# RetNet attention and a PReLU MLP in one kernel: masks and carries moved to ScalarE and GpSimd, one PReLU issued earlier, the copies of the running sums one gap later

## The chip, the cores and the metric

The kernel runs on one core of a Trainium2 chip. The core has TensorE (matmuls, called PE in the profile; PEld are its weight loads), VectorE (DVE), ScalarE (ACT), GpSimd (POOL) and SyncE (SP), whose queue issues nearly all the DMAs here. Each engine works through its own instructions in order; an instruction that must wait for another engine holds up everything behind it on its own. The metric is device time in microseconds of one execution.

## What is computed

The reference has two blocks. The first is a retention layer: 8 batches, 8 heads, 576 positions, head size 64. The second is an MLP over the 4608 tokens of 512 features that come out of it, with 2048 hidden features and a PReLU whose slope differs for each hidden feature.

```python
scores = scale * np.matmul(q, k.transpose(0, 1, 3, 2))
Dmat = np.where(rel >= 0, gamma[:, None, None] ** rel[None, :, :], 0.0)
ret = scores * Dmat[None, :, :, :]
return np.matmul(ret, v).astype(np.float32)
...
h = x @ w_in
g = np.maximum(h, 0.0) + alpha * np.minimum(h, 0.0)
return (g @ w_out).astype(np.float32)
```

Everything is 32-bit floating point. `Dmat` is a causal decay, a power of the head's `gamma` in the distance of two positions.

## The kernel before

**Attention in chunks.** The decay factors into a power for the row and one for the column, so q and v are scaled once, and a sequence of 576 is cut into 9 chunks of 64. Inside a chunk the scores are multiplied by a triangular 0/1 `mask`. What earlier chunks contribute is kept as a 64x64 state per head: the products of k and v of one chunk, summed over the chunks before it with a decay. Values are mask part plus state part.

**Batches after the first** are done by pair of heads, four pairs a batch. A pair has five steps: `scale_pair` (GpSimd scales q at L500, ACT scales v at L505), `transposes` (DVE, L511), `pair_scores` (PE L528, copies of q on ACT L531, masks on DVE L536), `pair_states` and `pair_values`. `pair_states` makes the products `pu` on PE (L547), copies the even ones on ACT (L552), forms the running sums `su` on DVE (L554, L558, L560), and in its last lines copies the sums into `vn` on ACT (L563), from where `pair_values` (PE L574) multiplies them. `su` has the one buffer of tag `kT`.

**The first batch** is done in three parts over all heads at once, two of four chunks and one of one chunk (`PARTS`). Part two is part number 1 in the code. For each part: `part_scale` (GpSimd, L595; argument 1 is q, 2 is v), `part_transposes` (PE L615, copies mostly on ACT L622; 0 is k, 1 is q), `part_scores` (PE L634, two masked copies out of PSUM on DVE at L638), `part_states` (PE L651, sums on DVE L661), `part_carry` (DVE L665: the last sum with the decay of a chunk, into the next part), `part_values` (PE L677 and L688, copies on ACT L693 and L695).

**The weights** come in 32 pieces of 512 KB, in the order in which the hidden units need them: for each of 8 units two pieces of `w_in` and two of `w_out`. The kernel reads both 32-bit halves of 64-bit numbers and builds 32-bit numbers from them. `piece_in` is the ACT half (L274, L276), into one of three buffers `wa`. `piece_out` is three DVE steps (L285, L288, L290) through one PSUM bank and an addition on GpSimd (L292); after it, `fetch` issues DMAs for a later piece, up to seven ahead, into a buffer whose old piece must have had its addition.

**The MLP** goes over blocks of 256 tokens. Each unit has two halves: hidden features (`ph`), PReLU, and the product with `w_out` (`po`, in `mlp_out`). Blocks 0 and 1 are done plainly: `plain_unit` is 16 matmuls (L395) into the single bank `psh0` and two Relus on ACT (L399, L401); `plain_relu` combines them on DVE (L411, two instructions), which also frees the bank; `mlp_out` is eight matmuls (L374). The other 16 blocks use a seven-product scheme of Strassen's kind (L439 and L359), whose weight sums `combine` makes on GpSimd (L302).

**The order of the work.** From the start up to the end of blocks 0 and 1, the order of instructions on each engine is that of the source (`tc.manual_schedule`). First come the parts of batch 0, with pieces of weights and the first four plain units between them. The names `part_...`, `piece_...`, `plain_unit(kb, i)` and `mlp_out` stand there one under another, and each puts its instructions at the tail of its engines' queues. Then a loop over twelve plain units has two places, the gaps, in which one entry of the list `steps` is worked off: "t" is `transposes`, "s" `pair_scores`, "u" `pair_states`, "p" `scale_pair`, "v" `pair_values` and the loads of the pair after the next. The list for a pair is:

```python
steps += [(("s", n),), (("u", n),), (("p", n + 1),), (("v", n), ("t", n + 1)), ()]
```

and the body of the loop, per unit: `plain_unit`, `plain_relu`, first gap, `piece_in`, `piece_out`, `mlp_out`, `combine`, `piece_in`, second gap, `piece_out`, `combine`. In the third of these units the first gap gets "s" and the second "u"; in later ones the entries follow on. After the loop, at about 160 us, the hand-written order is closed, and the rest (the other 24 attention pairs and the other blocks) is ordered by the framework from its source order and dependences.

Of the kernel before, what the change touches and what calls it, by code (L numbers as in the profile page):

```python
# [14 lines left out]
ALU = mybir.AluOpType  # L15
# [3 lines left out]
def kernel(  # L19
# [10 lines left out]
    nc = tc.nc  # L30
# [3 lines left out]
    P = 128  # L34

    NPAIR = H // 2
    C = 64
# [94 lines left out]

    def load_part(x):
        j0, j1 = PARTS[x]
        for i, src, eng in ((0, k, nc.sync), (1, q, nc.scalar if x == 0 else nc.sync),
                            (2, v, nc.sync)):
            for m in range((j1 - j0 + 1) // 2):
                s0 = (j0 + 2 * m) * C
                rows = min(P, j1 * C - s0)
                eng.dma_start(part[x][i][0:rows, m],  # L140
                              src[0, :, s0:s0 + rows].rearrange("h p d -> p h d"))

    load_part(0)
    a16 = const.tile([NFC, P], FP32, name="a16")
# [134 lines left out]
    def piece_out(n):  # L279
        for _ in range(min(n, len(half_done))):  # L280
            at, a, lo, hi, t = half_done.pop(0)
            dst = pieces[at][1]

            c = ps_h.tile([P, 2, HM], INT32, tag="psh1", name=f"wc_{at}")
            nc.vector.tensor_scalar(c.bitcast(FP32), a, HI_MIN, HI_MAX, ALU.max, ALU.min)  # L285


            nc.vector.tensor_scalar(c, c, 3, 0x3FFFFFF8,  # L288
                                    ALU.logical_shift_left, ALU.bitwise_and)
            nc.vector.scalar_tensor_tensor(out=dst.bitcast(INT32), in0=hi, scalar=-0x40000000,  # L290
                                           in1=c, op0=ALU.bitwise_and, op1=ALU.bitwise_or)
            nc.gpsimd.tensor_tensor(out=dst.bitcast(INT32), in0=dst.bitcast(INT32), in1=lo,  # L292
                                    op=ALU.add)
            free.append(t)
            fetch(at + 1 + AHEAD)
# [55 lines left out]
    def mlp_out():  # L351
        kb, i, g = pend.pop(0)
        if kb in PLAIN:
            return plain_out(kb, i, g)
        if i == 0:
            acc[kb] = [ps_o.tile([P, 2, HM], FP32, tag=f"pso{n}", name=f"po{n}_{kb}")
                       for n in range(4)]
        for n, (x, y) in enumerate(PROD):
            nc.tensor.matmul(acc[kb][n // 2][:, n % 2, :], g[:, x, :], w_out[i][:, y, :],  # L359
                             start=(i == 0 and n % 2 == 0),  # L360
                             stop=(i == NU - 1 and (n % 2 == 1 or n == 6)),
                             skip_group_check=True)
        if i == NU - 1:
            out_block(kb, acc.pop(kb))
# [42 lines left out]
    def plain_relu():  # L407
        kb, i, g, ph = relus.pop(0)
        for x in range(2):
            fc = x * NU + i  # L410
            nc.vector.scalar_tensor_tensor(  # L411
                out=g[:, 2 * x:2 * x + 2].rearrange("p m t -> p (m t)"),
                in0=g[:, 4 + 2 * x:6 + 2 * x].rearrange("p m t -> p (m t)"),
                scalar=nalpha[:, fc:fc + 1], in1=ph[:, x], op0=ALU.mult, op1=ALU.add)
        pend.append((kb, i, g))
# [125 lines left out]
    def pair_states(n, kn, vn):  # L541
        c = pairs[n][1]
        ps = [ps_tile([P, NM - 1, D], f"pu{p2}_{n}") for p2 in range(2)]
        for j in range(NJ - 1):
            for h2 in range(2):
                x = (h2, 1 - h2)[j % 2]
                nc.tensor.matmul(ps[j % 2][half(x), j // 2], kn[half(1 - h2), j],  # L547
                                 vn[half(1 - h2), h2, j], start=True, stop=True)
        su = attn.tile([P, S], FP32, tag="kT", name=f"su_{n}")[:, 0:S - D].rearrange(
            "p (j d) -> p j d", d=D)  # L550
        g1, g2 = gch[:, 0, c:c + 1], gch[:, 1, c:c + 1]
        nc.scalar.copy(su[:, 0::2], ps[0])  # L552
        for h2 in range(2):
            nc.vector.scalar_tensor_tensor(  # L554
                out=su[half(h2), 1::2], in0=su[half(h2), 0::2], scalar=g1[half(h2)],
                in1=ps[1][half(1 - h2)], op0=ALU.mult, op1=ALU.add)
        for j in range(3, NJ - 1, 2):
            nc.vector.scalar_tensor_tensor(out=su[:, j], in0=su[:, j - 2], scalar=g2,  # L558
                                           in1=su[:, j], op0=ALU.mult, op1=ALU.add)
        nc.vector.scalar_tensor_tensor(out=su[:, 2::2], in0=su[:, 1:NJ - 3:2], scalar=g1,  # L560
                                       in1=ps[0][:, 1:], op0=ALU.mult, op1=ALU.add)
        for h2 in range(2):
            nc.scalar.copy(vn[half(h2), h2, 1:], su[half(h2)])  # L563

# [24 lines left out]
    def part_scale(x, i):  # L589

        j0, j1 = PARTS[x]
        t = part[x][i]
        for m in range((j1 - j0 + 1) // 2):
            rows = min(P, (j1 - j0) * C)
            nc.gpsimd.tensor_tensor(  # L595
                out=t[0:rows, m], in0=t[0:rows, m],
                in1=tp[0:rows, i - 1, m, :, None].to_broadcast([rows, H, D]), op=ALU.mult)
# [26 lines left out]
    def part_scores(x):  # L624
        at = tat[x] = (mlp.tile([P, 8 * P], FP32, tag="g", name=f"pa_{x}") if x == 0 else
                       room(4, 0, 4)).rearrange("p (h n) -> p h n", h=2)
        banks = part_banks(x, 2 if x == 0 else None, "ps")
        kT, qT = tT[x, 0], tT[x, 1]
        for m in range(2):
            for c in range(NPAIR):  # L630
                for p2 in range(2):
                    for h2 in range(2):
                        j = chunk(2 * m + p2)
                        nc.tensor.matmul(banks[h2][half(p2), (2 * c + m) * C:(2 * c + m + 1) * C],  # L634
                                         kT[half(h2), c, j], qT[half(h2), c, j],
                                         start=True, stop=True)
        for h2 in range(2):
            nc.vector.tensor_tensor(  # L638
                out=at[:, h2].rearrange("p (n s) -> p n s", s=C),
                in0=banks[h2].rearrange("p (n s) -> p n s", s=C),  # L640
                in1=mask[:, None, :].to_broadcast([P, 8, C]), op=ALU.mult)

    def part_states(x):
        kn, vn = part[x][0], part[x][2]
# [17 lines left out]
            was = sums[x][j]  # L662

    def part_carry(x):
        nc.vector.tensor_tensor(out=carry[x + 1], in0=sums[x][3],  # L665
                                in1=gch[:, 2, :, None].to_broadcast([P, NPAIR, D]), op=ALU.mult)

    def part_values(x):
# [75 lines left out]
    part_scale(0, 2)  # L744
    part_scores(0)
    part_states(0)
    part_carry(0)
    piece_in(2)
    piece_out(2)
    part_values(0)  # L750
    aps = ps_a.tile([P, NFC], FP32, tag="psa", name="aps")
    nc.tensor.transpose(aps, a16, ident[0:NFC, 0:NFC])
    nc.vector.tensor_copy(alpha, aps)
    nc.vector.tensor_scalar(nalpha, alpha, -1.0, None, ALU.mult)
    piece_in(3)
    piece_out(1)
    part_scale(1, 1)
    piece_out(2)
    part_scale(1, 2)
    piece_in(1)  # L760
    plain_unit(0, 0)
    plain_relu()
    part_transposes(1, 0)
    part_transposes(1, 1)
    piece_out(1)
    mlp_out()
    piece_in(1)
    piece_out(1)
    part_scores(1)
# [28 lines left out]

    turned, mts = {}, {}

    def step(what, n):
        if what == "p":
            scale_pair(n)
        elif what == "t":
            turned[n] = transposes(n)
        elif what == "s":
            mts[n] = pair_scores(n, *turned.pop(n))
        elif what == "u":  # L810
            pair_states(n, loaded[n][0], loaded[n][3])
        elif what == "v":
            pair_values(n, loaded[n][3], mts[n])
            del loaded[n]
            loaded[n + 2] = load_pair(n + 2)
# [2 lines left out]
    last = 2 * NPAIR - 1  # L818
    steps = [(("t", NPAIR),)]
    for n in range(NPAIR, last + 1):  # L820
        steps += [(("s", n),), (("u", n),), (("p", n + 1),), (("v", n), ("t", n + 1)), ()]

    def gap():
        for x in steps.pop(0) if steps else ():
# [28 lines left out]
    for n, (b, c) in enumerate(pairs):  # L853
        if n <= last:
            continue
        if n == last + 1:
            pop_units(1)
        if n + 1 < len(pairs) and n + 1 not in loaded:
            loaded[n + 1] = load_pair(n + 1)
        kn, _, _, vn = loaded[n]  # L860
        share = -(-len(queue) // (NPAIR - c))
        cuts = [(share + i) // 3 for i in range(3)][::-1]
        kT, qT = turned.pop(n)
        mt = pair_scores(n, kT, qT)
        pop_units(cuts[0])
        pair_states(n, kn, vn)
        pop_units(cuts[1])
        if n + 1 < len(pairs):
            scale_pair(n + 1)
            turned[n + 1] = transposes(n + 1)  # L870
        pair_values(n, vn, mt)
        del loaded[n]
        pop_units(cuts[2])
        if c == NPAIR - 1:
            enqueue(b)
# [31 lines left out]
```

## Time and profile before

| | |
|---|---|
| median of 4 runs | 1029.34 us (1028.92 to 1029.66) |
| the profiled execution's own time | 1029.66 us |
| its span in the profile | 1027.9 us |
| PE busy | 1008.6 us, 98% of the span |
| DVE busy | 772.0 us, 75% |
| ACT busy | 266.8 us, 26% |
| POOL busy | 173.3 us, 17% |
| PE busy, 20 to 48 us | 24.59 us of 28.00 |
| PE busy, 48 to 77 us | 29.00 us of 29.00 |
| PE busy, 77 to 125 us | 46.47 us of 48.00 |
| PE busy, 125 to 160 us | 35.00 us of 35.00 |
| PE busy, 160 to 860 us | all of it |

A line of the timeline reads: start in us, time from the first to the last of the group in us, engine, line of the source, operation, what is written and read, shapes, count; in square brackets the idle time of that engine before it, and what ended that idle time. "issue" means that the profile shows nothing that the engine waited for. A wait for several engines is put down to the one whose event came last, so the name after the arrow can be that of an engine which had nothing to do with it.

### The profile page before, as it was taken

Reading aid. Unit: us, or ns where it says so; the run is one execution under the profiler, and the core shown is the slowest. Engines: PE = TensorE matmul, PEld = TensorE weight load, DVE = VectorE, ACT = ScalarE, POOL = GpSimd, SP = SyncE. Lnnn points to the kernel's source line nnn. Section 1 sums busy time; section 2 is a strip of 40 time slices with the busy share of each in tenths; the row PEclk is TensorE's granted clock in tenths of the full one; section 3 lists DMA queues with packets and bytes.
Section 4 is the critical chain, followed back from the end, with each engine's and each line's share of the span. In section 5 each row is a group of like instructions: output and inputs, shape, how many; then the busy total and the mean of one; then the engine's idle time right before and its main releaser. Section 6 shows DMA issues by size and latency. Waiting matters only on the chain.

```text
span 1027.9 us, 23097 instructions
## 1 busy us (share of the span) xinstructions
PE 1008.6 (98%) x9385; PEld 890.4 (87%) x9385; DVE 772.0 (75%) x2045; ACT 266.8 (26%) x597; POOL 173.3 (17%) x194
## 2 busy tenths in 40 slices
PE   5899999999999999999999999999999999999998
PEld 4666668998999999999999999999999999999997
DVE  7768877787877777777768787878788776667665
ACT  4456562222222222021122222222222211000000
POOL 4556665300200020100010000200020001010000
PEclk8999999999999999999999999999999999999999
DMA  9964654232222313112113122322222100000000
GB/s 248 248 168 133 167 90 105 42 68 51 64 48 47 68 36 67 25 45 36 45 35 68 36 61 42 68 38 66 48 47 56 24 22 2 21 1 21 1 21 22
DMA packets 229307, 64.30 MB, mean 63 GB/s; under 512 B 214336, under 2 KB 222544, under 8 KB 229200
## 3 DMA queue, kind: packets, MB, share of 16 engines
q1 hardware_dynamic: 227088, 62.29, 26.6%
q8 instruction: 74, 1.21, 0.5%
q10 hardware_dynamic: 2112, 0.53, 0.3%
q14 instruction: 33, 0.27, 0.1%
HBM read 53.35 MB, written 9.44 MB: 61 GB/s over the span
## 4 chain that ended last, share of the span: by engine, by line
PE 93%; DVE 2%; issue 1%; ACT 1%; DMA 1%; POOL 0%; SPq 0%; ACTq 0%; DVEq 0%; POOLq 0%
PE ph L439 40%; PE po L359 38%; PE ph L395 4%; PE po L374 3%; PE pv L574 3%; PE ps L528 2%; PE pu L547 2%; DMA w_out<-in_q_dram 1%; DVE mt L536 1%; DVE su L558 0%; PE pv L688 0%; PE pt L615 0%; DMA kx<-in_k_dram 0%; DVE wc L288 0%; PE ps L634 0%
## 5 line engine op out<-in xcount | busy, mean ns | idle before, releaser
L359 PE MATMUL po<-w_out,g 128*128 128x256 f32 x1792 | 407.8, 379 | 0.0
L359 PEld LDWEIGHTS po<-w_out,g 128*128 128x128 f32 x1792 | 330.8, 190 | 39.7
L450 DVE TENSOR_TENSOR g<-ph,g 128x256 f32<-128x256 f32 (+1 forms) x512 | 187.7, 387 | 184.6 <-ACT g L445 112.5
L439 PE MATMUL ph<-xb,w_in 128*128 128x128 f32 x2048 | 277.7, 279 | 0.0
L439 PEld LDWEIGHTS ph<-xb,w_in 128*128 128x128 f32 x2048 | 253.1, 192 | 8.2 <-issue 0.5
L439 PE MATMUL ph<-xt,w_in 128*128 128x128 f32 x1536 | 213.3, 275 | 0.0
L439 PEld LDWEIGHTS ph<-xt,w_in 128*128 128x128 f32 x1536 | 192.1, 192 | 0.0
L445 ACT COPY g<-ph 128x128 f32<-128x128 f32 x128 | 33.9, 265 | 397.4 <-PE ph L439 374.1
L461 DVE TENSOR_TENSOR g<-g 128x128 f32<-128x128 f32 x512 | 126.8, 289 | 7.8
L455 DVE SCALAR_TENSOR_TENSOR g<-g 128x512 f32<-128x512 f32 x128 | 91.7, 717 | 3.9
L453 DVE TENSOR_SCALAR g<-g,alpha 128x256 f32<-128x256 f32 x256 | 84.9, 374 | 3.7
L500 POOL TENSOR_TENSOR qx<-qx,tabx 128x576 f32<-128x576 f32 x28 | 32.9, 1174 | 309.5 <-DMA qx<-in_q_dram 263.6
L395 PE MATMUL ph<-xb,w_in 128*128 128x256 f32 x256 | 60.5, 390 | 3.1 <-ACT vn L100 1.2
L536 DVE SCALAR_TENSOR_TENSOR mt<-ps,th,mask 64x320 f32<-64x320 f32 (+1 forms) x112 | 57.8, 516 | 4.4 <-PE ps L528 2.6
L395 PEld LDWEIGHTS ph<-xb,w_in 128*128 128x128 f32 x256 | 49.0, 195 | 13.4 <-issue 3.4
L374 PE MATMUL po<-w_out,g 128*128 128x512 f32 x128 | 58.5, 599 | 0.6 <-DVE g L411 0.6
L425 POOL TENSOR_TENSOR xt<-xb 128x256 f32<-128x256 f32 x16 | 11.6, 727 | 215.1 <-PE ph L439 202.6
L425 POOL TENSOR_TENSOR xt<-xb,xt 128x256 f32<-128x256 f32 x32 | 23.6, 736 | 142.1 <-ACT xb L583 141.4
L563 ACT COPY vn<-su 64x512 f32<-64x512 f32 x56 | 34.5, 616 | 48.4 <-DVE su L560 47.7
L505 ACT ACTIVATE vn<-vn,tabv 64x576 f32<-64x576 f32 x56 | 43.3, 773 | 14.4 <-DMA vn<-in_v_dram 13.5
L374 PEld LDWEIGHTS po<-w_out,g 128*128 128x128 f32 x128 | 23.5, 190 | 24.7 <-issue 22.5
L583 ACT COPY xb<-pv 128x256 f32<-128x256 f32 (+3 forms) x84 | 22.7, 322 | 79.0 <-PE pv L574 79.0
(119 smaller groups left out, 684.9 us busy)
## 6 DMA issues: line engine op xcount, KB each, us to landing
out_dram<-osb SPq DMA_DIRECT2D x36, 256.0 KB, 2.3
kx<-in_k_dram SPq DMA_DIRECT2D x112, 72.0 KB, 2.7
qx<-in_q_dram SPq DMA_DIRECT2D x112, 72.0 KB, 2.5
vn<-in_v_dram SPq DMA_DIRECT2D x56, 144.0 KB, 3.1
kn<-in_k_dram SPq DMA_DIRECT2D x56, 144.0 KB, 3.2
raw<-in_moe_w_in_dram SPq DMA_DIRECT2D x24, 256.0 KB, 4.3
raw<-in_moe_w_out_dram SPq DMA_DIRECT2D x10, 512.0 KB, 4.7
w_in<-in_moe_w_out_dram SPq DMA_DIRECT2D x6, 512.0 KB, 5.0
```

The source lines that it names most:

```text
L359: nc.tensor.matmul(acc[kb][n // 2][:, n % 2, :], g[:, x, :], w_out[i][:, y, :], start=(i == 0 and n % 2 == 0), stop=(i == NU - 1 and (n % ...
L374: nc.tensor.matmul(acc[kb][m], g[:, 2 * x + m], w_out[i][:, 2 * x:2 * x + 2].rearrange("p x f -> p (x f)"), start=(i == 0 and x == 0), sto ...
L395: nc.tensor.matmul(ph[:, x], w_in[i // UST][:, cc // 2 * 2 + x, i % UST, cc % 2], xb[kb][:, cc], start=(cc == 0 and x == 0), stop=(cc == N ...
L425: nc.gpsimd.tensor_tensor(out=o, in0=x0, in1=x1, op=ALU.subtract)
L439: nc.tensor.matmul(ph[m][:, o], w_in[i // UST][:, l, i % UST, cc], r[:, cc], start=(n in (0, 3) and cc == 0), stop=(n in (2, 6) and cc == ...
L450: nc.vector.tensor_tensor(out=o, in0=x0, in1=x1, op=ALU.add)
L453: nc.vector.tensor_scalar(g[:, 4 + 2 * m:6 + 2 * m], g[:, 2 * m:2 * m + 2], 0.0, alpha[:, fc:fc + 1], ALU.min, ALU.mult)
L455: nc.vector.scalar_tensor_tensor(out=g[:, 0:4].rearrange("p x t -> p (x t)"), in0=g[:, 0:4].rearrange("p x t -> p (x t)"), scalar=0.0, in1 ...
L461: ins = nc.vector.tensor_tensor(out=g[:, o, :], in0=g[:, x0, :], in1=g[:, x1, :], op=op)
L505: nc.scalar.activation(vn[x, h2], vn[x, h2], ACTF.Copy, scale=tabv[x, c:c + 1])
L536: nc.vector.scalar_tensor_tensor(out=mt[to, h2, p2::2], in0=ps[p2][half(x), 0:nm], scalar=th[to, 3, h:h + 1], in1=mask[to, None, :].to_bro ...
L563: nc.scalar.copy(vn[half(h2), h2, 1:], su[half(h2)])
```

## The change

Five edits, all up to the end of the hand-written order.

1. `load_part` is rewritten; it issues the same DMAs from the same queues in the same order.
2. In `part_scores` of part two, the two masked copies on DVE become, for each, a plain copy out of PSUM on ACT and a multiplication by the mask in place on GpSimd. Part one is unchanged.
3. `part_carry` runs on GpSimd in place of DVE, and the first one is issued after the first two pieces rather than ahead of them.
4. Around the first plain unit the source order changes: the fourth piece's DVE and GpSimd half ahead of the scaling of q of part two; the fifth piece's, and the scaling of v, behind the unit's PReLU; the first `mlp_out` between the transposes of k and those of q, where it stood behind both and behind the sixth piece's half.
5. The two ACT copies of the running sums leave `pair_states` for a function `pair_sums`. In the loop of the plain units this is a step "w" of its own, in the gap after that of "u". In the rest of the kernel it follows at once, as before.

```diff
+        return su
+
+    def pair_sums(vn, su):
         for h2 in range(2):
             nc.scalar.copy(vn[half(h2), h2, 1:], su[half(h2)])
...
         for h2 in range(2):
-            nc.vector.tensor_tensor(
-                out=at[:, h2].rearrange("p (n s) -> p n s", s=C),
-                in0=banks[h2].rearrange("p (n s) -> p n s", s=C),
-                in1=mask[:, None, :].to_broadcast([P, 8, C]), op=ALU.mult)
+            to, fro = [t.rearrange("p (n s) -> p n s", s=C) for t in (at[:, h2], banks[h2])]
+            m = mask[:, None, :].to_broadcast([P, 8, C])
+            if x == 0:
+                nc.vector.tensor_tensor(out=to, in0=fro, in1=m, op=ALU.mult)
+            else:
+                nc.scalar.copy(to, fro)
+                nc.gpsimd.tensor_tensor(out=to, in0=to, in1=m, op=ALU.mult)
...
     def part_carry(x):
-        nc.vector.tensor_tensor(out=carry[x + 1], in0=sums[x][3],
+        nc.gpsimd.tensor_tensor(out=carry[x + 1], in0=sums[x][3],
                                 in1=gch[:, 2, :, None].to_broadcast([P, NPAIR, D]), op=ALU.mult)
...
     part_states(0)
-    part_carry(0)
     piece_in(2)
     piece_out(2)
+    part_carry(0)
     part_values(0)
...
     piece_in(3)
-    piece_out(1)
+    piece_out(2)
     part_scale(1, 1)
-    piece_out(2)
-    part_scale(1, 2)
     piece_in(1)
     plain_unit(0, 0)
     plain_relu()
+    piece_out(1)
+    part_scale(1, 2)
     part_transposes(1, 0)
+    mlp_out()
     part_transposes(1, 1)
     piece_out(1)
-    mlp_out()
     piece_in(1)
     piece_out(1)
     part_scores(1)
...
         elif what == "u":
-            pair_states(n, loaded[n][0], loaded[n][3])
+            sus[n] = pair_states(n, loaded[n][0], loaded[n][3])
+        elif what == "w":
+            pair_sums(loaded[n][3], sus.pop(n))
...
-        steps += [(("s", n),), (("u", n),), (("p", n + 1),), (("v", n), ("t", n + 1)), ()]
+        steps += [(("s", n),), (("u", n),), (("w", n), ("p", n + 1)), (("v", n), ("t", n + 1)), ()]
...
-        pair_states(n, kn, vn)
+        pair_sums(vn, pair_states(n, kn, vn))
```

## The prediction

> **What bounds the kernel now.** I read four views in this order: the page's shares, PE's timeline, the timelines of ACT and DVE where PE has a hole, and PE's timeline again for the first 45 us.
>
> The page first: the busy shares, and the instruction queue among the DMA queues.
>
> ```profile
> PE 1008.6 (98%) x9385; PEld 890.4 (87%) x9385; DVE 772.0 (75%) x2045; ACT 266.8 (26%) x597; POOL 173.3 (17%) x194
> q8 instruction: 74, 1.21, 0.5%
> ```
>
> PE is the bound, so only its holes can be won. A table of PE's busy time by stage puts them: 20 us to 48 us holds 24.59 us of work in 28.00, 77 to 125 holds 46.47 in 48.00, and 125 to 860 has none. What comes after 160 us therefore moves as a block. Nearly all that this change can win lies in the two early stages.
>
> PE's timeline around the larger hole of the second stage (start, us, then the group; in brackets the idle time before it):
>
> ```profile
> 105.92 3.62 PE L395 MATMUL ph<-xb,w_in 128*128 128x256 f32 x16
> 109.46 1.27 PE L574 MATMUL pv<-mt,vn 128*64 128x64 f32 x36
> 110.66 3.70 PE L374 MATMUL po<-w_out,g 128*128 128x512 f32 x8
> 115.54 3.69 PE L395 MATMUL ph<-xb,w_in 128*128 128x256 f32 x16 [1.18 <-ACT vn L100]
> 119.16 0.80 PE L528 MATMUL ps<-qT,kT 64*64 64x64 f32 x36
> 124.20 0.68 PE L547 MATMUL pu<-vn,kn 64*64 64x64 f32 x28 [0.35 <-DVE mt L536]
> 124.82 3.72 PE L395 MATMUL ph<-xb,w_in 128*128 128x256 f32 x16
> ```
>
> Ends are modelled, so I go by starts. From one unit's ph to the next takes 8.28 us with a value step between (90.29 less 82.01) and 8.53 with scores and states (82.01 less 73.48), where nothing waits. Here the same stretches take 9.62 (115.54 less 105.92) and 9.28 (124.82 less 115.54). The two holes are worth 1.34 + 0.75 = 2.09 us.
>
> Now ACT, then DVE, in the same stretch:
>
> ```profile
> 102.87 0.38 ACT L552 COPY su<-pu 128x256 f32<-128x256 f32 x1
> 108.20 1.26 ACT L563 COPY vn<-su 64x512 f32<-64x512 f32 x2 [4.96 <-DVE su L560]
> 109.49 0.68 ACT L274 ACTIVATE wa<-raw 128x512 f32<-128x512 f32 x1
> 111.88 1.56 ACT L505 ACTIVATE vn<-vn,tabv 64x576 f32<-64x576 f32 x2
> 113.35 0.57 ACT L399 ACTIVATE g<-ph 128x512 f32<-128x512 f32 x1
> ```
> ```profile
> 107.71 0.41 DVE L560 SCALAR_TENSOR_TENSOR su<-su,gch,pu 128x192 f32<-128x192 f32 x1
> 110.20 0.70 DVE L285 TENSOR_SCALAR wc<-wa 128x512 f32<-128x512 f32 x1 [2.09 <-ACT wa L274]
> 114.53 0.86 DVE L411 SCALAR_TENSOR_TENSOR g<-g,nalpha,ph 128x256 f32<-128x256 f32 x2
> 122.02 2.13 DVE L536 SCALAR_TENSOR_TENSOR mt<-ps,th,mask 64x320 f32<-64x320 f32 x4
> ```
>
> ACT stands 4.96 us before the copy of the sums with two pieces' casts queued behind it, so DVE then stands 2.09 us for a cast. The PReLU L411, which frees the one ph bank, ends at 115.39, 0.15 before PE starts. The row names L100, merely the last ACT event before; I read DVE as the gate. Masks L536 end at 124.15 and free the banks that pu needs: the second hole is the same delay.
>
> **The change part by part.**
>
> *Sums one gap later.* In gap A of the unit at 105.92 ACT goes from L552 (to 103.25) straight to the two pieces' casts, four instructions at about 0.57 a step, done by 105.6; their data were issued before 95.6 (SP's four at 89.66). The copies L563 still start when L560 ends (108.2 to 109.46), so values, which start at 109.46, do not wait more. Behind them L505 takes 1.56 (to 111.0), then L399 and L401 end at 112.1; ph had ended at 109.5. DVE goes on at 108.15 rather than 110.20: two pieces at 2.26 and 2.07 a step, L411 at 112.5 to 113.35. PE is ready at 105.92 + 8.28 = 114.20, so the hole goes. Next, transposes and two pieces take 0.78 + 0.84 + 2.23 + 2.06 as now; L411 at 119.17; masks end 3.02 later, 122.19. PE comes to pu at 114.20 + (123.52 less 115.54) = 122.18. Hole two goes with a few hundredths to spare: what is late next is DVE, with 42.25 us of work in what becomes 45.9. GpSimd gets the earlier piece at 110.4 for 112.49, so SP's refills behind its adds (the four issues at 104.85) come earlier, none later. The moves in the other three pairs cost nothing: there PE has no hole, and the copies end before values (in the first, ACT does L399 and L401 at 85.8 to 86.9, L563 to 88.1; values start at 89.09). Term: -2.09.
>
> *Early part: PReLU ahead, values masked elsewhere.* PE now:
>
> ```profile
> 28.47 3.70 PE L374 MATMUL po<-w_out,g 128*128 128x512 f32 x8 [0.59 <-DVE g L411]
> 35.65 3.18 PE L395 MATMUL ph<-xb,w_in 128*128 128x256 f32 x14 [0.83 <-issue]
> 38.76 1.16 PE L677 MATMUL pv<-w_out,w_out 64*64 64x64 f32 x64
> 39.85 0.79 PE L688 MATMUL pv<-w_out,w_out 64*32 64x64 f32 x50
> 41.57 1.15 PE L688 MATMUL pv<-w_out,w_out 64*32 64x64 f32 x78 [0.93 <-issue]
> 43.63 3.70 PE L374 MATMUL po<-w_out,g 128*128 128x512 f32 x8
> ```
>
> L411 need not follow the fifth piece: it starts when L401 ends, 27.29 for 27.94, and po at 27.82, 0.65 earlier; GpSimd's fourth add comes ahead of the scaling of q and ends at 27.1. But eight q transposes (0.95) now follow po, at 31.45 for about 26.9, and their ACT copies (0.5 each) stand open: scores at 32.68 for 32.10, +0.58. On ACT the seventh piece's casts are queued behind those copies: 33.1 for 29.08. DVE gets it at 33.8 for 30.97, sums L661 (1.84) to 37.75, eighth piece to 39.9, PReLU at 40.5 for 39.99.
>
> The masks leave DVE (1.29 for two) and become two ACT copies (0.58 each, row L622) and two GpSimd multiplies. No row shows a GpSimd mask; L595 has the shape, 1.02 each. GpSimd's line: fifth add to 31.55, scaling of v to 33.55, sixth to 34.85, seventh 35.98 to 37.28, masks 37.3 to 39.35, scaling of part three to 41.35, eighth to 42.65, carry to 43.2 (0.55; bounds 0.42, DVE's, and 0.73, L425). Values start at 39.4 for 38.76, and the second po needs the eighth add at about 43.4. The first carry frees 0.35 us of DVE, covered: PE's first unit waits for ACT's L695, which ends at 20.64. Bounds for a mask: 0.65 (DVE's) and 1.30 (the adds L292, same shape).
>
> [...] The rows say 1.02 against 0.65, 1.6 times. [...]
>
> Then the stalls called issue. Between the last two PE runs 14 + 64 + 50 = 128 matmuls, each with its weight load, so 256 instructions; the q8 packets are 16 KB each. I read them as blocks of PE's program arriving late: 3.5 us after the block before was entered (32.13 to 35.65), then 5.9 (35.65 to 41.57). The block is entered with scores, at 32.7, so the next comes at 36.2, and ph ends at 39.35. The one after comes between 36.2 + 3.5 = 39.7 and 36.2 + 5.9 = 42.1; PE reaches it at 41.2. So PE is at the second po 0.35 earlier to 0.55 later than now. I take 0, by the middle: SP's issues that crowd the queue come later too, those at 32.72 at 34.9 and that at 39.94 at 42.7.
>
> [...]
>
> Late SP issues are covered: the pieces of 32.72 are cast at 56.70 and 64.37, the pair loads of 40.32 (now 43.1) are first used at 65.63. The load helper's rewrite leaves the same DMAs in the same order: 0.
>
> *Sum.* -2.09 + 0 on the profiled execution's 1029.66 (span 1027.9) gives 1027.57. Its own time is 0.32 above the median 1029.34; for the median I say 1027.2.
>
> **The rivals.** (1) The early part eats much of it. If both late blocks take the longer 5.9 us, the first comes at 38.6, ph ends at 41.8, and the second block comes at 44.5 for 41.57: the second po is 2.95 late. With +0.6 to +2.95 the time is 1027.9 to 1030.2, within 0.2%. For it: the DMA engines are full from 20 to 48 us (share 0.99). Against: queued work thins as the adds that release it come later.
> (2) DVE becomes the bound in 77 to 125: L558's three take 1.47 us at 84.37 and 2.56 at 105.23; one more such spread (1.09) in a chain with hundredths of slack leaves half of the gain: 1028.3. Against: new GpSimd work does not lie in that stretch.
> (3) Slower: the order after 160 us is not written by hand, and a shifted start could give another. One hole like the 1.18 at each of 4 of the remaining 24 pairs costs 4.7: 1032.0. It decides from 4.15 (2.09 + 2.06). Against: 735 us without a hole, DVE at 75%.
>
> **How the numbers follow.** A measurement here tells about 0.2%, 2.06 us: faster means under 1027.28, slower over 1031.40. My case, 0.66: 1026.6 to 1027.9 by the bounds of the early term, split 0.48 faster, 0.18 same, as the median falls just beyond the line and PE's idle time in the two stages (3.41 + 1.53 us) leaves more room below. Rival 1: 0.12, rival 2: 0.08, both mostly same with 0.02 faster between them. Rival 3: 0.14, slower. So 0.50, 0.36, 0.14. The range runs from 1025.9 (both issue stalls gone too) to 1030.2, rival 1's end; rival 3 stays outside.
>
> **What would show it.** Right: no ACT wait over 2 us before the sums' copy near 103, no PE hole near 114 or 123, ph to ph 8.28 and 8.53 there; first po near 27.8, scores near 32.7, values near 39.4. Wrong: an issue stall over 1.5 us near 36 or 41, values waiting for GpSimd past 40, an L411 that still ends after po, or holes past 160 us.

## The result and the profile after

The changed kernel takes 1028.24 us (median of 39 runs, 1027.06 to 1029.51), the kernel before 1029.68 (59 runs, 1028.35 to 1032.67). The ratio is 0.9983 with a 95% interval of 0.9979 to 0.9988: between 1.2 and 2.2 us were won, most likely 1.75. The forecast was 1027.2. The gain is real, and smaller than the 0.2% that the forecast called faster.

The profiled execution of the changed kernel took 1029.49, with a span of 1027.8, hardly less than that of the kernel before. It is the second slowest of the 39, and its stages show why. The page, its first row:

```profile
PE 1008.7 (98%) x9385; PEld 891.3 (87%) x9385; DVE 769.2 (75%) x2041; ACT 267.5 (26%) x599; POOL 176.9 (17%) x198
```

PE's work is the same; only its holes can have changed. PE's timeline in the second stage (start, us, group; in brackets idle time and its releaser):

```profile
107.84 3.62 PE L394 MATMUL ph<-xb,w_in 128*128 128x256 f32 x16
111.39 1.27 PE L576 MATMUL pv<-mt,vn 128*64 128x64 f32 x36
112.59 3.70 PE L373 MATMUL po<-w_out,g 128*128 128x512 f32 x8
116.13 3.62 PE L394 MATMUL ph<-xb,w_in 128*128 128x256 f32 x16
119.67 0.80 PE L527 MATMUL ps<-qT,kT 64*64 64x64 f32 x36
...
124.03 0.69 PE L546 MATMUL pu<-vn,kn 64*64 64x64 f32 x32
124.66 3.72 PE L394 MATMUL ph<-xb,w_in 128*128 128x256 f32 x16
```

Both holes are gone: 116.13 less 107.84 is 8.29, for 9.62 before, and 124.66 less 116.13 is 8.53, for 9.28. ACT and DVE show what opened them:

```profile
104.80 0.38 ACT L551 COPY su<-pu 128x256 f32<-128x256 f32 x1
105.20 0.70 ACT L273 ACTIVATE wa<-raw 128x512 f32<-128x512 f32 x1
...
109.45 1.26 ACT L565 COPY vn<-su 64x512 f32<-64x512 f32 x2 [1.87 <-DVE su L559]
```
```profile
108.96 0.41 DVE L559 SCALAR_TENSOR_TENSOR su<-su,gch,pu 128x192 f32<-128x192 f32 x1
109.28 0.69 DVE L284 TENSOR_SCALAR wc<-wa 128x512 f32<-128x512 f32 x1
...
113.59 0.86 DVE L410 SCALAR_TENSOR_TENSOR g<-g,nalpha,ph 128x256 f32<-128x256 f32 x2
...
121.81 2.13 DVE L535 SCALAR_TENSOR_TENSOR mt<-ps,th,mask 64x320 f32<-64x320 f32 x4
```

The casts of the two pieces now stand ahead of the copies on ACT. ACT waits 1.87 in place of 4.96, and DVE goes from the sums straight to a piece (109.28), where it stood 2.09 before. The PReLU L410 ends at 114.45, 1.7 before PE wants the bank. The masks L535 end at 123.94, and `pu` starts at 124.03: the slack there is under a tenth.

PE and GpSimd in the early stage:

```profile
22.47 5.54 PE L394 MATMUL ph<-xb,w_in 128*128 128x256 f32 x16 [1.14 <-ACT xb L700]
27.84 1.04 PE L617 MATMUL pt<-ident,w_out 128*128 128x128 f32 x8
29.79 3.67 PE L373 MATMUL po<-w_out,g 128*128 128x512 f32 x8 [0.91 <-DVE g L410]
...
34.63 1.18 PE L636 MATMUL ps<-w_out,w_out 64*64 64x64 f32 x64 [0.29 <-ACT w_out L624]
...
40.54 0.33 PE L682 MATMUL pv<-w_out,w_out 64*64 64x64 f32 x2
41.76 1.16 PE L682 MATMUL pv<-w_out,w_out 64*64 64x64 f32 x62 [0.90 <-POOL w_out L646]
42.85 1.71 PE L693 MATMUL pv<-w_out,w_out 64*32 64x64 f32 x128
```
```profile
37.96 1.29 POOL L291 TENSOR_TENSOR w_out<-w_out,raw 128x512 int32<-128x512 int32 x1 [1.18 <-ACT wa L273]
39.21 2.50 POOL L646 TENSOR_TENSOR w_out<-w_out,mask 128x512 f32<-128x512 f32 x2
...
44.91 0.60 POOL L670 TENSOR_TENSOR w_out<-w_out,gch 128x256 f32<-128x256 f32 x1
```

Neither of the two waits called issue (0.83 and 0.93) is there. In their place the values wait 0.90 for the second mask on GpSimd. The first ph started at 22.47, for 20.79 before: that is where this execution lost most of what it won later.

For every kernel below I use the same cuts. *Start* is the start of the first ph, *first unit* runs from there to the transposes behind it, *early* from these transposes to the second po, and *pairs* from the second po to the ph at the end of the stage (124.82 before, 124.66 here; it follows the states of the loop's third pair, though the expectations below say the fourth). What remains of the span behind these is 903.08 to 903.15 us in each row, so the four columns hold the whole difference. Each row is one profiled execution.

| kernel | start | first unit | early | pairs |
|---|---|---|---|---|
| before | 20.79 | 5.17 | 17.67 | 81.19 |
| changed | 22.47 | 5.37 | 17.72 | 79.10 |
| e1 sums only | 20.38 | 5.95 | 16.61 | 79.11 |
| e2 early part only | 22.00 | 5.01 | 17.70 | 81.20 |
| e3 masks back on DVE | 20.43 | 5.11 | 18.05 | 79.10 |
| e4 old order around the unit | 20.43 | 6.23 | 16.92 | 79.10 |
| e5 changed again | 20.80 | 5.61 | 17.69 | 79.10 |
| e6 copies on GpSimd, not moved | 20.50 | 4.91 | 18.56 | 79.10 |
| e7 both transposes first | 20.61 | 5.14 | 15.96 | 79.10 |
| e9 shorter prefetch | 20.91 | 5.01 | 17.06 | 79.10 |
| e10 v scaled earlier | 20.59 | 4.91 | 19.08 | 79.10 |
| e11 e7 again | 20.40 | 6.29 | 15.80 | 79.10 |
| e12 quiet queue | 21.18 | 6.12 | 15.99 | 79.10 |

### The profile page after: what moved, and what is told of

The parts are those of the page before. It is cut to its first block, busy times and chain, and to the rows that moved or that the text cites. A ratio compares the mean times of both kernels' runs of the same rounds, so it can differ in the third digit from the quotient of the medians.

```text
span 1027.8 us, 23098 instructions
## 1 busy us (share of the span) xinstructions
PE 1008.7 (98%) x9385; PEld 891.3 (87%) x9385; DVE 769.2 (75%) x2041; ACT 267.5 (26%) x599; POOL 176.9 (17%) x198
## 3 DMA queue, kind: packets, MB, share of 16 engines
q8 instruction: 74, 1.21, 0.5%
## 4 chain that ended last, share of the span: by engine, by line
PE 97%; DVE 1%; DMA 1%; issue 1%; ACT 0%; POOL 0%; ACTq 0%; DVEq 0%; POOLq 0%
PE ph L438 40%; PE po L358 38%; PE po L373 6%; PE ph L394 5%; PE pv L576 3%; PE ps L527 2%; PE pu L546 2%; DMA w_out<-in_q_dram 1%; PE pv L693 0%; PE pv L682 0%; PE ps L636 0%; DVE w_out L666 0%; PE pt L617 0%; DVE wc L284 0%; DVE pa L643 0%
## 5 line engine op out<-in xcount | busy, mean ns | idle before, releaser
L535 DVE SCALAR_TENSOR_TENSOR mt<-ps,th,mask 64x320 f32<-64x320 f32 (+1 forms) x112 | 57.8, 516 | 4.5 <-PE ps L527 2.7
```

Source lines behind the costliest of these rows:

```text
L535: nc.vector.scalar_tensor_tensor(out=mt[to, h2, p2::2], in0=ps[p2][half(x), 0:nm], scalar=th[to, 3, h:h + 1], in1=mask[to, None, :].to_bro ...
```

## The experiments

### The two halves of the change alone

e1 is the kernel before with the copies moved and nothing else; e2 is the changed kernel with the copies back in the gap of "u".

```diff
-        steps += [(("s", n),), (("u", n),), (("p", n + 1),), (("v", n), ("t", n + 1)), ()]
+        steps += [(("s", n),), (("u", n),), (("w", n), ("p", n + 1)), (("v", n), ("t", n + 1)), ()]
```

> The kernel before with the sums' copies one gap later and nothing else. Theory A (the whole gain is ACT's queue in the units at 106 and 116 us): time -2.1 us against before, ratio 0.9980; in the profile no hole on PE between 77 and 125 us, second po to the ph after the fourth pair's states 79.1 us where before shows 81.19; the stretch from the first ph to the second po stays 22.8. Rival B (the early edits carry half of the gain or more): -0.9 us or less, ratio 0.9991 or more.

```diff
-        steps += [(("s", n),), (("u", n),), (("w", n), ("p", n + 1)), (("v", n), ("t", n + 1)), ()]
+        steps += [(("s", n),), (("u", n), ("w", n)), (("p", n + 1),), (("v", n), ("t", n + 1)), ()]
```

> The changed kernel with the sums' copies back in the gap of the states: only the early edits. Theory A: +0.3 us against before (0 to +0.6), ratio 1.0003, the two holes near 115 and 124 us back (about 2 us), first ph to second po 23.1. Rival B: -0.9 us, ratio 0.9991. Rival C (the early edits, the first carry above all, also make the first ph later, which the profile of the changed kernel shows at 22.47 for 20.79): first ph again near 22.4, +1.7 us.

e1: 1027.33 us, ratio 0.9974 (0.9965 to 0.9983). e2: 1030.24, ratio 0.9998 (0.9989 to 1.0007). So the copies carry the gain, and the other four edits together changed nothing that could be measured. PE of e2 has both holes back where they were:

```profile
116.62 3.69 PE L394 MATMUL ph<-xb,w_in 128*128 128x256 f32 x16 [1.18 <-ACT vn L100]
...
125.29 0.68 PE L546 MATMUL pu<-vn,kn 64*64 64x64 f32 x28 [0.35 <-DVE mt L535]
```

The pairs stage is 81.20 in e2 and 79.11 in e1: 2.09 apart, to a hundredth the term of the forecast. The first ph of e2 came at 22.00, so e2 alone leaves its rival C open; e5 below answers it. In e1, PE waits in the early stage as in the kernel before, and the timeline again calls the wait issue:

```profile
38.62 0.79 PE L691 MATMUL pv<-w_out,w_out 64*32 64x64 f32 x50
40.89 1.14 PE L691 MATMUL pv<-w_out,w_out 64*32 64x64 f32 x78 [1.47 <-issue]
```

It is after the 50th matmul of that line again. That wait was 0.93 before, in the same code up to here: its size belongs to the execution, its place to the program.

### Is it ACT's queue? Copies on another engine, unmoved; copies later still

e6 leaves the copies where they were and gives them, in the loop of the plain units, to GpSimd. If the wait at the head of ACT's queue was the cause, that frees the casts too.

```diff
-            nc.scalar.copy(vn[half(h2), h2, 1:], su[half(h2)])
+            if eng is None:
+                nc.scalar.copy(vn[half(h2), h2, 1:], su[half(h2)])
+            else:
+                eng.tensor_copy(vn[half(h2), h2, 1:], su[half(h2)])
...
-            pair_states(n, loaded[n][0], loaded[n][3])
+            pair_states(n, loaded[n][0], loaded[n][3], nc.gpsimd)
```

> The kernel before with the two copies of the sums in their old place in the order, but on GpSimd, in the four pairs of the hand-written loop. Theory A (what cost 2.09 us is the work queued behind the waiting copies on ACT): the holes close as when the copies move, second po to the ph 79.1, ratio 0.998, provided GpSimd's own queue, which then waits 5 us for the sums with a piece's addition and the scaling of q behind it, does not make anything late. Rival G (it is VectorE's chain of sums itself that is late, wherever the copies are): 81.2, no gain.

Measured 1027.67, ratio 0.9981 (0.9972 to 0.9990), pairs 79.10. ACT and GpSimd:

```profile
103.21 0.38 ACT L552 COPY su<-pu 128x256 f32<-128x256 f32 x1
103.61 0.70 ACT L274 ACTIVATE wa<-raw 128x512 f32<-128x512 f32 x1
...
107.63 1.27 POOL L566 COPY vn<-su 64x512 f32<-64x512 f32 x2 [0.86 <-ACT vn L505]
```

ACT goes straight on to the casts, as it does when the copies are moved. The gain is the same with the copies at the old place in the source on another engine. What held PE was the order on ACT's queue, as forecast, and GpSimd has room for the copies in this stage (busy for 34.84 of the 48 us from 77 to 125).

e8 is e1 with the copies two gaps later, in the gap of the values that read them.

```diff
-        steps += [(("s", n),), (("u", n),), (("w", n), ("p", n + 1)), (("v", n), ("t", n + 1)), ()]
+        steps += [(("s", n),), (("u", n),), (("p", n + 1),), (("w", n), ("v", n), ("t", n + 1)), ()]
```

> The kernel before with the sums' copies two gaps later, at the head of the step that multiplies them. Theory A (the copies are only a matter of ACT's order: behind the sums they must come before values, ahead of the casts they must not): PE now waits at values for copies behind ACT's casts or PReLU halves, 2.5 to 4 us in each of the four pairs, so 8 to 12 us more than one gap later, 1036 to 1040 us, with the ACT waits before L563 gone. Rival G: no more than 1 us from before.

Measured in one run 1044.96, over the upper end of what was expected. PE, and then windows over it (us; busy time and count of PE, PEld, DVE, ACT, POOL; granted clock; DMA share; GB/s):

```profile
91.67 0.34 PE L577 MATMUL pv<-mt,vn 128*64 128x64 f32 x4
93.84 0.33 PE L577 MATMUL pv<-mt,vn 128*64 128x64 f32 x2 [1.84 <-ACT vn L566]
94.48 1.14 PE L577 MATMUL pv<-mt,vn 128*64 128x64 f32 x30 [0.31 <-ACT vn L566]
95.56 5.41 PE L395 MATMUL ph<-xb,w_in 128*128 128x256 f32 x16
...
118.18 0.33 PE L577 MATMUL pv<-mt,vn 128*64 128x64 f32 x2 [1.43 <-ACT vn L566]
...
167.06 0.33 PE L577 MATMUL pv<-mt,vn 128*64 128x64 f32 x2 [1.43 <-ACT vn L566]
```
```profile
95.56:98.97 3.41, 3.41 (x10) 2.73 (x9) 2.32 (x4) 1.03 (x4) 1.98 (x3) 0.53 0.39 110
98.97:119.60 20.63, 18.89 (x157) 12.76 (x157) 16.19 (x29) 12.54 (x22) 11.38 (x11) 1.00 0.62 148
119.60:123.10 3.50, 3.50 (x16) 1.84 (x12) 2.17 (x4) 2.87 (x9) 3.00 (x4) 0.51 0.55 159
```

Each of four pairs loses PE a wait of 1.74 to 2.15 us. The price of the wait is not all: behind the first the granted clock was 0.53 from 95.56 to 98.97 and 1.00 after that, and the ph took 5.41 for 3.62. Three such stretches lie behind the first three waits (0.53, 0.51 and 0.50), and one at the second po (0.50 from 44.50 to 47.90), ahead of the first late copy. From the start of the slow ph to the next group took 5.24 us (95.56 to 100.80), where the ph at 133.60 of the same run has 3.56, so 1.7 more; four such stretches cost 6.8 by my estimate, and the waits themselves are 7.8. The sum, 14.6, is most of the 16.65 by which e8 takes longer than e1 from the first ph to the first matmul of the Strassen blocks; from there to the end both take 870.96 to 870.98. The stretch at the second po is not the copies' doing, so by this estimate about 15 of the 16.65 us are. I had priced the waits and not the clock. So the gap behind that of the sums is the right place for the copies, and the next one, which they share with the values that read them, is the wrong one.

### The early part taken to pieces

e3 is the changed kernel with the masks of part two on DVE again. e4 is the changed kernel with the old source order around the first plain unit, the masks staying on ACT and GpSimd.

```diff
-            if x == 0:
+            if True:
                 nc.vector.tensor_tensor(out=to, in0=fro, in1=m, op=ALU.mult)
```

> The changed kernel with the masks of part two on VectorE again. Theory A (GpSimd's two mask multiplies at 1.25 us are what values wait for, 0.90 us in the profile): -0.8 us against the changed kernel, ratio to before 0.9975; values follow ph at once, the PReLU of the second unit starts 1.3 us later behind masks and the eighth piece without holding po. Rival D (VectorE then is the one that is late, as the PReLU and the eighth addition hold the second po): +0.5 us against the changed kernel, ratio 0.9988.

```diff
     piece_in(3)
-    piece_out(2)
+    piece_out(1)
     part_scale(1, 1)
+    piece_out(2)
+    part_scale(1, 2)
     piece_in(1)
     plain_unit(0, 0)
     plain_relu()
-    piece_out(1)
-    part_scale(1, 2)
     part_transposes(1, 0)
-    mlp_out()
     part_transposes(1, 1)
     piece_out(1)
+    mlp_out()
```

> The changed kernel with the old order around the first plain unit (fifth piece ahead of the PReLU, transposes of q ahead of the first po), masks on ACT and GpSimd, carries on GpSimd, sums later. Theory A (the new order loses more by the open copies of the transposes than the earlier PReLU wins): scores 0.4 to 0.6 us earlier after the first ph than in the changed kernel, masks done before ph ends, first ph to second po 22.8, time -0.3 us against the changed kernel, ratio to before 0.9980. Rival E (the earlier PReLU is a gain): +0.5 us, ratio 0.9988.

e3: 1027.49, ratio 0.9967 (0.9955 to 0.9980). e4: 1027.50, ratio 0.9970 (0.9959 to 0.9982). Both intervals overlap that of e1 and, at its edge, that of the changed kernel, so the times do not settle what either edit costs. They do speak against rivals D and E, which had the edits as gains: 0.9988 lies outside both intervals. The rows say more. PE of e3:

```profile
34.37 0.70 PE L394 MATMUL ph<-xb,w_in 128*128 128x256 f32 x2
35.60 3.29 PE L394 MATMUL ph<-xb,w_in 128*128 128x256 f32 x14 [0.53 <-issue]
...
39.91 0.79 PE L693 MATMUL pv<-w_out,w_out 64*32 64x64 f32 x50
41.52 1.16 PE L693 MATMUL pv<-w_out,w_out 64*32 64x64 f32 x78 [0.82 <-issue]
```

With the wait for GpSimd gone, the issue waits stand there instead, 0.53 and 0.82, and the early stage is 18.05 for 17.72. In this execution the slower masks would have cost next to nothing, since PE stands there anyway (for its own program, as I read it in the section on late blocks). e4 shows the same: no wait for a mask, 0.18 and 1.47 for issue.

e5 is the changed kernel once more, with no edit, for its late start.

> The changed kernel itself, once more, on the chip of the three runs beside it. Theory F (the late first ph of its profile, 22.47 us for 20.79, is the spread of single executions in the first 20 us, where PE's instruction stream is that of before): first ph anywhere from 20.4 to 22.5, second po to the ph after the fourth pair's states 79.1 again, ratio to before 0.998. Rival C (the late start belongs to this kernel's code): first ph again at 22 or later.

Measured 1028.02, ratio 0.9982 (0.9973 to 0.9991). The first ph started at 20.80, so the 22.47 was that execution's own. Before that ph PE has an issue wait, 2.93 in the profile of before and 3.97 in the changed one; over all profiles here the first ph starts between 20.38 and 22.47, whether the early code is the old or the new. The early stage, though, is 17.72, 17.70 (e2) and 17.69 in the three executions that have this code, where the old early code gave 17.67, 16.61, 18.56, 16.38 (e8) and, with a shorter prefetch, 17.06 and 15.99. Where GpSimd's masks set the time it is steady; where the program sets it, it is not.

### A better early order

e7 takes the order of the changed kernel and puts both transposes ahead of the first `mlp_out` again (PE then does not wait at po for the PReLU), and the pieces' DVE and GpSimd halves so that GpSimd reaches the masks sooner.

```diff
     piece_in(3)
-    piece_out(2)
+    piece_out(1)
     part_scale(1, 1)
+    piece_out(1)
     piece_in(1)
...
     part_transposes(1, 0)
-    mlp_out()
     part_transposes(1, 1)
+    mlp_out()
     piece_out(1)
     piece_in(1)
-    piece_out(1)
     part_scores(1)
+    piece_out(1)
```

> The changed kernel with both transposes of part two ahead of the first po, the PReLU still ahead of the fifth piece, and the scores, copies and masks ahead of the seventh piece. Theory H (in the early part the block of PE's program that is loaded at about 39 to 42 us after the start sets the second po, and whatever comes earlier waits for it): scores about 1 us earlier after the first ph than in the changed kernel, values no longer wait for GpSimd, but an issue wait of 1.5 us or more stands ahead of the second po and the stretch from the first ph to it stays 22.5 to 23.1; ratio to before 0.9972, the same as with the sums alone. Rival I (the masks and the order set it): the stretch falls to 21.5 or less, 1 us better than with the sums alone.

Measured 1026.29, ratio 0.9971 (0.9960 to 0.9982); e5, the changed kernel in the same comparison, had 1028.02 (1027.18 to 1028.79, against 1025.65 to 1027.55 here). The early stage is 15.96, which is 1.73 less than that of e5 (17.69). The medians lie 1.73 apart too; that they agree to the hundredth is chance, as the stages are those of one execution each. PE:

```profile
31.23 1.16 PE L636 MATMUL ps<-w_out,w_out 64*64 64x64 f32 x64
...
33.47 0.69 PE L656 MATMUL pu<-w_out,w_out 64*64 64x64 f32 x32 [0.31 <-POOL w_out L597]
34.10 3.72 PE L394 MATMUL ph<-xb,w_in 128*128 128x256 f32 x16
...
38.84 1.95 PE L693 MATMUL pv<-w_out,w_out 64*32 64x64 f32 x128
41.71 3.70 PE L373 MATMUL po<-w_out,g 128*128 128x512 f32 x8
```

The timeline marks no issue wait, though PE comes to its values 1.3 us earlier than in e5. The trace has a gap of 0.23 after the 50th of the 128 matmuls, at the place of the waits seen before; the 128 take 1.95 for 1.71 in the changed profile. The states wait 0.31 for the scaling of v. I had thought that late blocks of PE's program would take back what an earlier order gives. In this execution they took 0.2 of it, so that theory fell here. e7 moves several things at once, and no run tells which of them wins.

e10 is e7 with the scaling of v one step earlier, for these 0.31.

```diff
     plain_relu()
-    piece_out(1)
     part_scale(1, 2)
+    piece_out(1)
     part_transposes(1, 0)
```

> The run with both transposes first, with the scaling of v ahead of the fifth piece's addition on GpSimd, for which states waited there (scores at 31.23, states only at 32.47 to 34.10). The theory that the masks and the order set the early part: states follow scores, ph 0.7 us earlier, the stretch from the first ph to the second po 20.4 us for 21.10, time -0.7 us against that run. The theory that a block of PE's program is next in line: an issue wait of 0.5 us or more comes back ahead of the second po, and the stretch stays at 21 us.

e11 is e7 again, with no edit.

> The run with both transposes of part two first, once more, as a yardstick on the same chip: stretch from the first ph to the second po 21.1 us again, ratio to before 0.9965 to 0.9975; if the first time was chance (a block that happened to come early), an issue wait of 0.5 us or more and a stretch over 22 us.

e10: 1026.20, ratio 0.9963 (0.9952 to 0.9975). e11: 1025.92, ratio 0.9958 (0.9946 to 0.9970). In e10 the states do follow the scores without a wait, and the ph behind them starts at 33.02. In the median it gains nothing. In the profiled execution the next thing in line is the program:

```profile
33.02 0.70 PE L394 MATMUL ph<-xb,w_in 128*128 128x256 f32 x2
35.98 4.87 PE L394 MATMUL ph<-xb,w_in 128*128 128x256 f32 x14 [2.27 <-issue]
```

That execution (1028.52, the slowest of its five) also ran the 14 matmuls at a granted clock of 0.64 between 36.00 and 40.78. Why the other four gain nothing is not shown. e11 repeats e7's gain: this order is faster than the kernel before and, by 1.73 in the one comparison that holds both, faster than the changed kernel. Against e1, the copies moved alone, no comparison holds both. Beside e11 ran e9 (below), which has e1's early order and e1's ratio, and it was slower by 1.30.

### Why the blocks come late: not settled

That the issue waits are waits for PE's program is my reading of the traces. They hold each packet of q8, the queue that the profile calls instruction (74 packets, 1.21 MB, so 16 KB each). In the profile of before three of them landed at 16.10, 34.26 and 40.18, and PE went on at 17.50, 35.65 and 41.57, each time 1.39 or 1.40 later. In e10 a packet landed at 34.52, and the wait of 2.27 ended at 35.98. Every issue wait named here ended 1.2 to 1.7 us after such a landing. What follows asks why the packets come so late.

The DMA engines are full in the early stage (share 0.99 from 20 to 48 us before), so I asked whether the refills of weights delay the loading of PE's program. e9 is e1 with four pieces ahead in place of six (behind the addition of a piece, `fetch` goes up to the sixth after it, not the seventh).

```diff
-    AHEAD = 6
+    AHEAD = 4
```

> The kernel before with the sums' copies one gap later (as in the run with that alone) and pieces fetched four ahead in place of six, so that SP issues the 1 MB of refills that stood at 33.5 us only after 40 us. Theory J (the second late block of PE's program waits behind these refills in the DMA engines): the issue wait of 1.47 us near 40 us falls under 0.5 us, the stretch from the first ph to the second po from 22.56 to 21.1 to 21.6 us, time 0.9 to 1.4 us less than with the sums alone (ratio to before about 0.9962), unless a piece then comes late. Rival K (the load takes its time whatever else is moved): the issue wait stays 0.9 us or more and the ratio 0.9974.

Measured 1027.22, ratio 0.9974 (0.9963 to 0.9984), the same as e1. PE waits 1.15 for issue at the same matmul:

```profile
40.92 1.15 PE L691 MATMUL pv<-w_out,w_out 64*32 64x64 f32 x78 [1.15 <-issue]
```

It did not test the point: SP put the loads of the first pair (from 34.13 on) where the refills had been. e12 therefore also ties the refill of one later piece, and with it SP's whole queue, to the last matmul of part two's values.

```diff
-                nc.sync.dma_start(to, src)
+                ins = nc.sync.dma_start(to, src)
+                if at == 12 and i == 0:
+                    tc.add_manual_dep(ins.ins, values[1].ins.name, ...)
```

> The sums' copies one gap later, pieces fetched four ahead, and the first refill that stood near 33 us made to wait for the last matmul of part two's values, so that SP, which issues in order, sends nothing between about 32 us and then. Theory J (the late blocks of PE's program wait behind refills in the DMA engines): the issue wait ahead of the second half of values, 1.47 and 1.15 us in the two runs before it, falls under 0.5 us; from the transposes after the first ph to the second po 15.6 to 16.1 us for 16.61; time 0.5 to 1 us less than with the sums alone, ratio to before 0.9962 to 0.9970, unless the later refills make a cast wait. Rival K (a block takes its 5 to 6 us whatever is moved beside it): the issue wait stays 0.9 us or more.

Measured 1026.58, ratio 0.9973 (0.9963 to 0.9984). SP's queue, and PE:

```profile
32.35 1.02 SPq L256 DMA_DIRECT2D raw<-in_moe_w_out_dram  x2
42.44 1.44 SPq L256 DMA_DIRECT2D raw<-in_moe_w_in_dram  x2
```
```profile
35.86 3.18 PE L400 MATMUL ph<-xb,w_in 128*128 128x256 f32 x14 [0.35 <-issue]
...
41.23 1.14 PE L696 MATMUL pv<-w_out,w_out 64*32 64x64 f32 x78 [0.38 <-issue]
```

SP issued nothing from 33.4 to 42.44, and the waits are short, 0.35 and 0.38, in agreement with the theory. But the ratio is that of e9, and the packets do not bear the theory out. From the start of the one block's packet to that of the next it took 5.92 us before, 6.65 in e1, 6.38 in e9 and 5.32 in e12; but in e7 and e11, where SP issued refills from 34.70 and 35.65 on, 5.36 and 5.12, and in the changed profile 4.14. So the quiet queue did no better than some executions with refills. Nor were the DMA engines idle at once: in e12 their share was 1.03 from 35 to 38 us and 0.15 from 38 to 41 (a packet counts whole where it starts). These packets took 1.0 to 1.5 us once they had started; what sets their start stays open.

## Why the prediction was right or wrong

*Sums one gap later, -2.09: right in place, cause and size.* Pairs 81.19 to 79.10 between the two profiles, and 79.10 or 79.11 in every one-gap or GpSimd kernel against 81.20 in e2. The step "ACT stands before the copy with two pieces' casts queued behind it" is shown by e6. "DVE is the gate, not L100" fits the two rows of DVE: the step L285 came 2.09 late before, and the same step, now L284, stands straight behind the sums. In the code ph does not touch the `vn` that L100 fills; no run holds the two apart. "A few hundredths to spare" at the second hole was 0.09. No engine hid a cost there: DVE is busy 43.9 of the 48 us from 77 to 125, for 42.25.

*Early part, 0: the sum right in the profiles, its composition wrong.* Early is 17.72 for 17.67; counted from the first ph to the second po, 23.09 and 23.30 (e5) for 22.84. Taken from the start of the transposes (25.96 before, 27.84 here), po came 1.95 later (forecast 27.82 less 25.96, so 1.86) and scores 6.79 (6.72), so the order on PE, DVE and ACT was read rightly. Three terms were off:
- *The mask on GpSimd* took 1.25, not the 1.02 of the scaling that I took for its nearest row; the bound of 1.30 from the adds L292 was nearer. Values could not run in full until 13.92 after the transposes, against a forecast of 13.44. Values waiting for GpSimd past 40 us was one of the prediction's own signs of being wrong, and it came: 41.76 in the changed profile, 40.31 in e5. Against the 0.645 of a mask on DVE (1.29 for two), 1.25 is 1.94 times, where the row of the scaling gave 1.6.
- *The issue waits*, forecast as 0.35 earlier to 0.55 later, were not there at all, as PE came to the blocks late enough: their packets had landed at 34.98 and 39.05, and PE came to them at 37.00 and 43.42. The two errors cancelled, and that the sum came out is luck. e3 shows how: without the masks on GpSimd, issue waits of 0.53 and 0.82 take the place of the 0.90.
- *The carry*, forecast 0.55, took 0.60 and nobody waited for it.

*The rivals.* (1), two late blocks, did not occur in the changed kernel, but 2.27 in e10 shows that the size was no fancy. (2), DVE as the bound: fell, PE has 48.00 of 48.00 us in that stage. (3), another order after 160 us: fell, the 903.1 us behind the stage are the same throughout. Yet 1028.24 lies beyond the 1026.6 to 1027.9 of the main case, in the band given to rival 1 and beside the 1028.3 of rival 2, without the mechanism of either.

*The time.* 1027.2 was 1.0 too low. Of that, 0.34 is the base: four runs gave 1029.34 as the median before, 59 gave 1029.68. The rest, 0.65, is that the medians differ by 1.44 where the terms said 2.09 (the ratio says 1.75, with 2.09 still inside its interval). The pairs term being exact, what is missing, if it is more than scatter, lies ahead of the pairs, where the forecast put the early part at 0. By the times that part costs 0.2 (e2 against the kernel before) to 0.9 (the ratios of the changed kernel and of e1); e2's interval, -1.1 to +0.7 us, holds the zero. The early stage is 17.69 to 17.72 in the three profiles of this code and 16.38 to 18.56 in the four of the old code with the full prefetch, so its size is not settled. The bounds of the early term, 0.35 earlier to 0.55 later, give 1026.9 to 1027.8; the wider 1026.6, and the range's lower end of 1025.9, are not worked out in the prediction. A forecast of 2.09 could not tell on which side of a line at 2.06 the time would come out, and the chances of 0.50 and 0.36 were too far apart for that.

## What to carry to other kernels

On an engine that works in order, look at what stands behind a waiting instruction, not at what the instruction itself costs: a copy that waited 4.96 us cost its reader nothing and PE 2.09 us. Move such a copy behind the work that others wait for, but keep it a gap ahead of its reader: in the reader's own gap it cost some 15 us, in the one run made. A stage with issue waits, as the early one here, need not pay for work taken off an engine in it (18.05 us with the masks back on DVE, for 17.72), and its time must be read from several executions, as one scatters by more than the change is worth (16.38 to 18.56 with the old code).

## What the runs showed of the hardware

Some waits of PE were followed by a stretch at half the granted clock. In e8 the clock was 0.50 from 44.50 to 47.90 us, 0.53 from 95.56 to 98.97, 0.51 from 119.60 to 123.10 and 0.50 from 143.50 to 146.90, and 1.00 in the stretches between these, from 41 to 160, each figure a mean over its stretch. Just ahead of the four PE had waited 1.20 and 0.27 us, 1.84 and 0.31, 1.43 and 0.31, 1.82 and 0.31. In e10 the clock was 0.64 from 36.00 to 40.78, behind a wait of 2.27, and 1.00 from 33 to 36 and from 40.78 to 44.

Such waits do not decide alone. The same 1.43 and 0.31 us stand ahead of the last values of the loop in e8 (167.06 and 167.71), and the clock was 1.00 from 165 to 180. Waits of 1.47 and 0.27 us in e1 left it at 1.00 from 40.90 to 46.50, and 1.47 and 0.28 in e4 from 41 to 47. What else decides stays open.

The issue waits of PE stood at the same places in every profile that has them: behind the 14th matmul of the second half of part one's values, the 2nd of the second unit's ph, and the 50th of the second half of part two's values, the last two 128 matmuls apart. They ranged from none (changed) to 2.27 us (e10) in the early stage and from 2.59 (e4) to 3.97 us (changed) before the first ph, in executions of nearly the same code. The clock was at half speed around the first ph, 0.50 from 17.30 to 24.13 before and from 19.39 to 26.21 in the changed profile, and the first unit goes with how much of it fell in there: 5.17 us before, 3.34 of them at half clock, and 5.37 in the changed profile, 3.74 of them. The 0.20 between the units is half of the 0.40 between these shares. In the table the first unit takes 4.91 (e6, e10) to 6.29 (e11). With the issue waits this makes up most of the scatter between the profiled executions: behind the pairs stage they agree within 0.07 us.
